# The last batch's dispatch weights made with tokens on the partitions, and the slots turned in two copies

## The chip, the cores and the metric

The kernel runs on one core of a Trainium2 chip. The metric is the device time of one execution in microseconds (us). The engines are TensorE (PE; its weight loads are PEld), VectorE (DVE), ScalarE (ACT), GpSimd (POOL) and SyncE (SP), which issues nearly all DMAs.

## The reference

Attention over 4 batches of 576 tokens, then a soft mixture of experts over all 2304 tokens, then an MLP with a Mish activation. What matters here is the dispatch of the mixture: each of the 32 slots takes a softmax over all tokens (over `axis 0`), and the slots' inputs are the weighted sums of the tokens.

```
x = attention(q, k, v)                      # (2304, 512)
logits = x @ phi                            # (2304, 32): a column for each slot
d = exp(logits - logits.max(0))             # maximum and sum run over the tokens
d /= d.sum(0) + 1e-9
slot_input = d.T @ x                        # (32, 512), 4 slots for each of 8 experts
h = relu(slot_input[e] @ w1[e]); slot_out[e] = h @ w2[e]
c = exp(logits - logits.max(1)); c /= c.sum(1) + 1e-9
y = c @ slot_out
out = (h2 * tanh(softplus(h2))) @ w_out     # h2 = y @ w_in
```

## The kernel before

The work runs in 16 periods, one for each pair of heads, in an order written out by hand (`PLAN`; `TAIL` for the last pair). Every recorded instruction of these stages keeps its place in its engine's queue, so an instruction that waits holds up all that stands behind it. After every fourth pair a batch is complete: its logits stand in `c_all[:, b]` with 128 tokens on the partitions, in 5 tiles of 32 slots (the fifth holds 64 tokens).

The softmax over tokens is kept running over the batches. For a batch the logits are turned on PE (`lt_pe`, tile `m_lt`, two halves), so that the 32 slots lie on the partitions; DVE takes their maxima (`lt_max`, tile `nM`, kept negated); ACT takes the exponentials and sums them (`lt_exp`, tile `lt`); DVE brings the running sum up to date (`lt_sum`, `asum`); PE turns the weights back (`d_pe`, tile `m_d`), and a copy takes them to `d`. `slots_pe` makes the weighted sums of the tokens (tile `m_si`: four products on `xg`, four on the rest `xr`, each in a quarter of the array's columns) and spreads the old sums' factor to 128 partitions (`m_al`). `slots_sum` adds them to the running slots in `acc`.

For the first three batches this lies inside the attention of the next batch. For the last one nothing is left beside it: the experts wait for the slots. The slots in `acc` are turned by four products (tile `m_sit`) and copied to `si_t`, which GpSimd has cleared. Then `h_ps` takes `si_t` times `w1`, 128 products in quarters of the array; after each, SP issues a load of a quarter of a `w2` matrix into the place of the weights just read (`quarter`). `rows_max`, `rows_less`, `rows_exp` make the combine weights of the last batch. `warm` issues products that nobody reads.

A single precision product of this kind stands in the trace as two records, a transposition as one.

Of the kernel before, what the change touches and what calls it, by code (L numbers as in the profile page):

```python
# [7 lines left out]
F32 = mybir.dt.float32  # L8
F32R = mybir.dt.float32r
U32 = mybir.dt.uint32  # L10
AF = mybir.ActivationFunctionType
ALU = mybir.AluOpType
# [30 lines left out]


TAIL = (
    "E8 y0 t5 T6 K1 T7 t6 k1 t7 R rA rD Q X0 qA qD B0 ca0 z1 w0 B1 B2 B3 B4 La la x1 Y1 X1 y1 ca1 Lb lb w1"
).split()


# [4 lines left out]
def kernel(  # L54
# [13 lines left out]
    nc = tc.nc  # L68
    NB, H, S, D = q.shape
    E, DM, F1 = w1.shape  # L70
    NSLOT = phi.shape[1]
# [3 lines left out]
    R = S - 512  # L75
    SCALE = 1.0 / float(D) ** 0.5
    KDM = DM // 128
# [7 lines left out]
    ps_m = psx.enter_context(tc.tile_pool(name="ps_m", bufs=4, space=PSUM))  # L85
# [11 lines left out]
    pe, act, dve, pool_, sp = (InOrder(e) for e in (nc.tensor, nc.scalar, nc.vector, nc.gpsimd, nc.sync))  # L97

    cs = const.tile([128, C_END], F32, name="cs")
    ident = cs[:, C_ID:C_ID + 128]  # L100
    rr = cs[:, C_RR:C_RR + 128]
    ii = cs[:, C_RR:C_RR + NSLOT]
# [4 lines left out]
    c_all = const.tile([128, NB, 5, NSLOT], F32, name="c_all")  # L107
    acc = const.tile([128, DM], F32, name="acc")

    nM = [const.tile([NSLOT, 3], F32, name=f"nM{i}") for i in range(2)]  # L110
    asum = const.tile([NSLOT, 2], F32, name="asum")
    asum4 = const.tile([128, 2], F32, name="asum4")
# [62 lines left out]
    def refill(keys):  # L175

        new = []
        for key in keys:
            room = parts.pop(key)
            if order[0][0] < 3:  # L180
                new.append(order.pop(0))
                parts[new[-1]] = room
            elif room[1][0] in (ra, rd):
                rooms.append(room[1])
        return new
# [25 lines left out]
    am = att.enter_context(tc.tile_pool(name="am", bufs=1))  # L211
# [15 lines left out]
    zs = [am.tile([128, 10, 2], F32, name=f"z{i}") for i in range(2)]  # L227
    sums = am.tile([NSLOT, 3], F32, name="sums")
    esum = sums[:, 1:3]
    tmps = [am.tile([128, 2 + i, 2, NSLOT], F32, name=f"tmp{i}") for i in range(2)]  # L230

    dma = sp.dma_start
# [10 lines left out]
    def load_pair(p, which="qk", dma=dma):  # L243
        b, h = divmod(2 * p, H)
        for nm in which:
            src = q if nm == "q" else k
            t = work(2, 2 * "qk".index(nm) + p % 2, (2, 256))
            dma(out=t, in_=src[b, h:h + 2, 0:512, :].rearrange("h (p c) d -> p h (c d)", c=4))
            raw[nm, p] = t
# [334 lines left out]
    dmat = {}  # L584

    def warm(pool, tag, n):

        ps = pool.tile([128, 128], F32, tag=tag, name="warm")
        for _ in range(n):
            tc.keep_in_program_order(nc.tensor.matmul(ps, lhsT=ident, rhs=ident, start=True, stop=True))  # L590

    def xtile(b, t):
        if t < 4:
            return xg[b, t // 2][:, t % 2, :]
        return xg[b, 2][:, :]
# [3 lines left out]
    def rows_max(b):  # L599
        st = rst[b] = am.tile([128, 5, 1], F32, tag="rst", name="rst")  # L600
        c = c_all[:, b]
        dve.tensor_reduce(out=st, in_=c, axis=AX.X, op=ALU.max)

    def rows_less(b):
        c = c_all[:, b]
        (dve if b == NB - 1 else pool_).tensor_tensor(out=c, in0=c, in1=rst[b].to_broadcast([128, 5, NSLOT]),
                                                      op=ALU.subtract)

    def rows_exp(b):
        act.activation(out=c_all[:, b], in_=c_all[:, b], func=AF.Exp)  # L610
# [27 lines left out]
    def lt_exp(b, i):  # L638
        new, nxt = nM[b % 2], nM[(b + 1) % 2]
        cur, old = nxt[:, 2:3], new[:, 2:3]  # L640
        if i == 0:
            dmat[b] = am.tile([NSLOT, S], F32, tag="lt", name="lt")
        o, n = HALVES[b][i]
        act.activation(out=dmat[b][:, o:o + n], in_=dmat.pop(("s", b, i))[:, 0:n], func=AF.Exp, bias=cur,
                       accum_out=esum[:, i:i + 1])
        if i and b:
            act.activation(out=asum[:, 0:1], in_=old, func=AF.Exp, scale=-1.0, bias=cur)

    def lt_sum(b):
        if b:  # L650
            dve.tensor_scalar(out=sums[:, 0:1], in0=asum[:, 1:2], scalar1=asum[:, 0:1], scalar2=None, op0=ALU.mult)
        dve.tensor_reduce(out=asum[:, 1:2], in_=sums[:, 0 if b else 1:3], axis=AX.X, op=ALU.add)

    def d_pe(b):
        lt = dmat.pop(b)
        ps = dmat["d", b] = ps_m.tile([128, 5, NSLOT], F32, tag="m", name="m_d")
        for t in range(5):
            n = 128 if t < 4 else R
            pe.transpose(ps[0:n, t, :], lt[:, t * 128:t * 128 + n], ident[0:NSLOT, 0:NSLOT])

    def d_copy(b, on, t0=None):
        if ("D", b) not in dmat:
            dmat["D", b] = am.tile([128, 5, NSLOT], F32, tag="d", name="d")
        d, ps = dmat["D", b], dmat["d", b]
        if on == "d" or t0 == 0:
            (dve.tensor_copy if on == "d" else act.copy)(d[:, 0:4], ps[:, 0:4])
        else:
            act.copy(d[0:R, 4], ps[0:R, 4])

    def slots_pe(b):  # L670
        dmat.pop(("d", b))
        d = dmat.pop(("D", b))
        al = None
        if b:
            al = ps_m.tile([128, 2], F32, tag="m", name="m_al")
            pe.matmul(al, lhsT=rr[0:NSLOT, :], rhs=asum, start=True, stop=True)
            dve.tensor_copy(asum4, al)
        ps = ps_m.tile([128, DM], F32, tag="m", name="m_si")
        for t in range(4):
            pe.matmul(ps[32 * t:32 * t + 32, :], lhsT=d[:, t, :], rhs=xtile(b, t), start=True, stop=False)  # L680
        for t in range(4):
            cols = slice(t * 128, (t + 1) * 128)
            pe.matmul(ps[32 * t:32 * t + 32, cols], lhsT=d[0:R, 4, :], rhs=xtile(b, 4)[:, cols],
                      start=False, stop=True)
        dmat["z", b] = ps
        for g in range(3):
            xg.pop((b, g))

    def slots_sum(b):
        ps = dmat.pop(("z", b))  # L690
        if b:
            n = DM // (2 if b == NB - 1 else 1)
            for o in range(0, DM, n):
                x, y = acc[:, o:o + n], ps[:, o:o + n]
                dve.scalar_tensor_tensor(out=x, in0=x, scalar=asum4[:, 0:1], in1=y, op0=ALU.mult, op1=ALU.add)
        else:
            dve.tensor_copy(acc, ps)

    pool_.memset(c_all, 0.0)
    dma(out=cs[:, C_COS:C_END], in_=cst[:, C_COS:C_END])  # L700
    load_pair(0, "k", act.dma_start)
    dma(out=cs[:, 0:C_COS], in_=cst[:, 0:C_COS])
# [200 lines left out]
    b = NB - 1  # L903
    ends = {"La": lambda: lt_pe(b, 0), "la": lambda: lt_max(b, 0), "Lb": lambda: lt_pe(b, 1), "lb": lambda: lt_max(b, 1)}
    for period in range(1, NP):
        for name, n in plan:
            p = period - n
# [6 lines left out]
    for name in TAIL:  # L914
        if name in ends:
            ends[name]()
        else:
            steps[name](NP - 1)
    warm(ps_m, "m", 6)
    lt_exp(b, 0)  # L920
    lt_exp(b, 1)
    lt_sum(b)
    d_pe(b)
    warm(ps_m, "m", 1)
    d_copy(b, "a", 4)
    d_copy(b, "a", 0)
    slots_pe(b)
    rows_max(b)
    rows_less(b)
    rows_exp(b)  # L930
    slots_sum(b)
    warm(ps_m, "m", 3)
    att.close()
    psx.close()

# [6 lines left out]
    ps_m = pse.enter_context(tc.tile_pool(name="ps_m2", bufs=6, space=PSUM, reuse_waits="tile"))  # L942

    si_t = p4.tile([128, KDM, 288], F32, name="si_t")
# [9 lines left out]
    for key in [take(rb, f"w{i}") for i in range(NRB)]:  # L954
        fetch(key)

    ps = ps_m.tile([128, KDM, NSLOT], F32, tag="m", name="m_sit")
    for c in range(KDM):
        nc.tensor.matmul(ps[:, c, :], lhsT=acc[:, c * 128:(c + 1) * 128], rhs=ii, start=True, stop=True)
    nc.vector.tensor_copy(  # L960
        si_t.rearrange("p c (e x) -> p c e x", x=36)[:, :, :, 0:4], ps.rearrange("p c (e j) -> p c e j", j=4)
    )

    warm(ps_m, "m", 1)

    rows_sum(b)
    rows_scale(b)
# [53 lines left out]
    for eg in range(2):  # L1021
        for hf in range(2):
            end = eg == 1 and hf == 1
            rows = [parts[1, 4 * eg + g, hf][0] for g in range(4)]
            new = refill([(1, 4 * eg + g, hf) for g in range(4)])
            for cc, fh in [(cc, fh) for cc in range(2) for fh in range(2)] if not end else [(0, 0), (1, 0), (0, 1), (1, 1)]:
                c = 2 * hf + cc
                for g in range(4):
                    e = 4 * eg + g
                    tc.keep_in_program_order(nc.tensor.matmul(  # L1030
                        h_ps[fh][32 * g:32 * g + 32, :], lhsT=si_t[:, c, 32 * e:32 * e + 32],
                        rhs=rows[g][:, cc * F1 + fh * 512:cc * F1 + fh * 512 + 512],
                        start=(eg == 0 and c == 0), stop=(eg == 1 and c == KDM - 1),
# [60 lines left out]
    for eg in range(2):  # L1094
        for hf in range(2):
            for cc in range(4):
                c = 4 * hf + cc
                for g in range(4):
                    e = 4 * eg + g
                    tc.keep_in_program_order(nc.tensor.matmul(  # L1100
                        so_ps[32 * g:32 * g + 32, :], lhsT=h_t[eg][:, c, 32 * g:32 * g + 32],
                        rhs=parts[2, e, hf][0][:, cc * DM:(cc + 1) * DM],
                        start=(eg == 0 and c == 0), stop=(eg == 1 and c == F1 // 128 - 1),
# [9 lines left out]
    for n, copy in ((0, nc.vector.tensor_copy), (2, nc.scalar.copy)):  # L1113
        ps = ps_m.tile([128, 2, 128], F32, tag="m", name="m_sot")
        for c in range(2):
            pin(nc.tensor.matmul(ps[:, c, :], lhsT=so_sb[:, (n + c) * 128:(n + c + 1) * 128], rhs=rr, start=True,
                                 stop=True))
# [395 lines left out]
    for u in range(len(units) + 2):  # L1513

        lag = 1 if u < UL else 2
        i, j = units[u] if u < len(units) else (None, None)
# [96 lines left out]
```

## Time and profile before

| | us |
|---|---|
| median of 3 runs | 581.66 |
| the 3 runs | 581.66, 581.52, 582.77 |
| the profiled execution's own time | 583.26 |
| its span, first to last instruction | 581.5 |
| mean granted clock of TensorE over the span | 0.996 |

The profiled execution took 1.76 us more than its span, and 1.60 us more than the median of the runs. A granted clock of 1.00 is 2.4 GHz, one of 0.50 is 1.2 GHz. The page gives busy time for each engine, a chain that is followed back from the last instruction, and groups of instructions. The rows below are from the stretch between the last pair of heads (to about 316 us) and the first expert products (from 325 us).

### The profile page before, as it was taken

The page shows a single profiled execution, that of the slowest core. Times are in us where ns is not written, and L with a number is a line of the kernel's source. Part 1 is how long each engine was busy: PE and PEld are TensorE (multiplying, and loading weights), DVE is VectorE, ACT ScalarE, POOL GpSimd, SP SyncE. Part 2 cuts the span into 40 slices and gives each one's busy share as a digit, 9 for nine tenths or more (in the row PEclk, how much of TensorE's full clock was granted, in tenths as well). Part 3 has the DMA queues.
Part 4 walks back from the last instruction along what each step waited for, and adds up shares of the span by engine and source line. Part 5 has one row for each costly group of instructions (what it writes and reads, how often), then busy time and mean ns, then how long its engine had stood idle before and what let it go on. Part 6 is the DMA issues. An engine that isn't in the chain of part 4 may idle for free.

```text
span 581.5 us, 12009 instructions
## 1 busy us (share of the span) xinstructions
PE 569.0 (98%) x4277; PEld 467.4 (80%) x4277; DVE 423.8 (73%) x867; ACT 389.1 (67%) x846; POOL 316.0 (54%) x399
## 2 busy tenths in 40 slices
PE   8899999999999999999998999999999999999996
PEld 7788887879888888878886435777788899999996
DVE  6787887988888878887574252999987756566564
ACT  4788887978888778886773032776757656556562
POOL 3968877689877777784000310000000078999993
PEclk9999999999999999999999999999999999999999
DMA  8599789999999888959877999642103010100112
GB/s 225 145 242 237 216 221 275 238 284 277 287 285 259 265 266 244 265 156 325 244 291 263 328 385 385 231 159 96 37 1 109 2 37 1 38 26 11 37 23 52
DMA packets 60475, 108.53 MB, mean 187 GB/s; under 512 B 13056, under 2 KB 26752, under 8 KB 60032
## 3 DMA queue, kind: packets, MB, share of 16 engines
q1 hardware_dynamic: 60144, 107.50, 61.7%
q8 instruction: 34, 0.56, 0.4%
q10 hardware_dynamic: 272, 0.26, 0.1%
q14 instruction: 25, 0.20, 0.1%
HBM read 70.25 MB, written 9.96 MB: 138 GB/s over the span
## 4 chain that ended last, share of the span: by engine, by line
PE 92%; DVE 4%; ACT 2%; DMA 1%; issue 1%; DVEq 0%; ACTq 0%
PE o_ps L1415 17%; PE s L95 15%; PE m_av L95 14%; PE o_ps L1313 14%; PE t L95 11%; PE hp L1238 3%; PE m_lg L95 3%; PE h_ps L1030 2%; PE so_ps L1100 2%; PE m_x L95 1%; PE m_q L95 1%; PE tk L95 1%; PE m_k L95 1%; PE m_si L95 1%; PE warm L590 1%; DMA w<-in_k_dram 1%
## 5 line engine op out<-in xcount | busy, mean ns | idle before, releaser
L1382 POOL TENSOR_TENSOR gr<-gr 128x128 f32<-128x128 f32 x81 | 59.8, 740 | 128.9 <-ACT gr L1378 124.5
L95 DVE TENSOR_REDUCE nmax<-s 128x1 f32<-128x576 f32 x144 | 107.0, 752 | 25.2 <-PE s L95 22.4
L95 ACT ACTIVATE P<-s,nmax 128x576 f32<-128x576 f32 x144 | 107.3, 746 | 17.3 <-DVE nmax L95 15.9
L95 PE MATMUL s<-qk_st 128*128 128x288 f32 x320 | 102.3, 337 | 1.9 <-ACT P L95 1.4
L1415 PE MATMUL o_ps<-ts,gr 128*128 128x256 f32 x480 | 97.5, 280 | 0.0
L95 POOL TENSOR_TENSOR w<-w,cs 128x512 f32<-128x512 f32 (+2 forms) x75 | 87.0, 1179 | 4.6 <-DMA w<-in_k_dram 2.6
L95 PE MATMUL s<-k_st,qk_st 128*128 128x288 f32 x320 | 89.1, 295 | 0.0
L95 PE MATMUL t<-cs,P 128*128 128x128 f32 x576 | 84.0, 273 | 0.0
L1415 PEld LDWEIGHTS o_ps<-ts,gr 128*128 128x128 f32 x480 | 80.0, 189 | 0.0
L95 PEld LDWEIGHTS s<-qk_st 128*128 128x128 f32 x320 | 60.3, 189 | 16.0 <-issue 9.1
L95 POOL TENSOR_TENSOR w<-w 128x256 f32<-128x256 f32 (+2 forms) x86 | 65.2, 779 | 13.6 <-ACT P L95 10.6
L95 ACT COPY PT<-t 128x512 f32<-128x512 f32 (+1 forms) x111 | 61.0, 558 | 14.0 <-PE t L95 12.5
L95 PEld LDWEIGHTS t<-cs,P 128*128 128x128 f32 x576 | 67.9, 142 | 1.4 <-DVE partl L95 0.6
L1415 PE MATMUL o_ps<-wo_h,gr 128*128 128x256 f32 x240 | 63.6, 283 | 0.0
L95 PEld LDWEIGHTS s<-k_st,qk_st 128*128 128x128 f32 x320 | 60.6, 190 | 0.0
L95 PE MATMUL m_av<-PT,w 128*64 128x320 f32 (+1 forms) x384 | 52.0, 411 | 0.0
L1313 PE MATMUL o_ps<-wo_h,gh 128*128 128x512 f32 x128 | 50.1, 394 | 0.0
L1313 PE MATMUL o_ps<-wo_l,gh 128*128 128x512 f32 x128 | 50.0, 393 | 0.0
L95 POOL TENSOR_TENSOR c_all<-c_all,tmp 128x64 f32<-128x64 f32 (+1 forms) x44 | 22.1, 502 | 50.3 <-DVE tmp L95 48.6
L1415 PEld LDWEIGHTS o_ps<-wo_h,gr 128*128 128x128 f32 x240 | 45.0, 188 | 0.2
L1398 DVE TENSOR_TENSOR gr<-gr 128x896 fp32r<-128x896 f32 (+2 forms) x28 | 31.4, 1122 | 17.4 <-ACT gr L1388 17.4
L95 PEld LDWEIGHTS m_av<-PT,w 128*64 128x64 f32 x384 | 25.8, 137 | 18.4 <-ACT PT L95 1.3
(208 smaller groups left out, 1192.1 us busy)
## 6 DMA issues: line engine op xcount, KB each, us to landing
w<-in_moe_w_dram SPq DMA_DIRECT2D x23, 1024.0 KB, 6.7
w<-in_moe_w_dram SPq DMA_DIRECT2D x36, 256.0 KB, 5.3
w<-in_moe_w_in_dram SPq DMA_DIRECT2D x16, 512.0 KB, 5.9
qk_st<-parth SPq DMA_DIRECT2D x45, 144.0 KB, 4.0
qk_st<-partl SPq DMA_DIRECT2D x45, 144.0 KB, 3.7
room<-in_moe_w_out_dram SPq DMA_DIRECT2D x12, 512.0 KB, 3.4
w<-in_q_dram SPq DMA_DIRECT2D x16, 256.0 KB, 4.3
w<-in_k_dram SPq DMA_DIRECT2D x15, 256.0 KB, 4.4
```

The lines of the kernel that those rows point to most:

```text
L95: return lambda *a, **k: tc.keep_in_program_order(f(*a, **k))
L590: tc.keep_in_program_order(nc.tensor.matmul(ps, lhsT=ident, rhs=ident, start=True, stop=True))
L1030: tc.keep_in_program_order(nc.tensor.matmul(h_ps[fh][32 * g:32 * g + 32, :], lhsT=si_t[:, c, 32 * e:32 * e + 32], rhs=rows[g][:, cc * F1 + ...
L1100: tc.keep_in_program_order(nc.tensor.matmul(so_ps[32 * g:32 * g + 32, :], lhsT=h_t[eg][:, c, 32 * g:32 * g + 32], rhs=parts[2, e, hf][0][: ...
L1238: pin(nc.tensor.matmul(hp[:, x * 256:x * 256 + 256], lhsT=wst[:, f * 128:(f + 1) * 128], rhs=ct[:, i * 256:(i + 1) * 256], start=True, sto ...
L1313: pin(nc.tensor.matmul(ops[i, n], lhsT=g_[:, cols], rhs=w_[f], start=(j == 0 and (x, k) == (0, 0)), stop=(j == NG - 1 and all(y[0] != n fo ...
L1382: pin(eng.tensor_tensor(out=o, in0=x, in1=y, op=op))
L1398: pin(nc.vector.tensor_tensor(out=l[:, x:y], in0=ga[u][:, 128 + x:128 + y], in1=h[:, x:y].bitcast(F32), op=ALU.subtract))
L1415: pin(nc.tensor.matmul(ops[p], lhsT=lhs, rhs=rhs, start=first, stop=(j == NG - 1 and k == 2)))
```

## The change

For the last batch alone, the logits are no longer exponentiated with slots on the partitions and turned back. The negated maxima of the 32 slots are spread to all 128 partitions by one product (`m_nm`: the maxima as weights, repeated 128 times, times a unit matrix). DVE adds them to `c_all` and ACT takes the exponentials in place, with the tokens on the partitions as the products of `m_si` need them. The slots' sums over the tokens are then made by GpSimd over the 5 tiles (`dsum`), copied four times side by side (`dsum4`) and summed over the partitions by a product with ones (`m_e`). The eleven `warm` products from `lt_pe` to `h_ps` become four. In `TAIL`, the step `w1` (scaling the last tokens into `xg` and `xr`) comes before `lb` (the maxima of the second half). The turned slots are made and copied in two parts, two column blocks by ACT and two by DVE.

```diff
-... ca1 Lb lb w1"
+... ca1 Lb w1 lb"
...
+    def last_weights(b):
+        new, nxt = nM[b % 2], nM[(b + 1) % 2]
+        cur, old = nxt[:, 2:3], new[:, 2:3]
...
+        warm(ps_m, "m", 1)
+        nm = ps_m.tile([128, NSLOT], F32, tag="m", name="m_nm")
+        pe.matmul(nm, lhsT=cur.to_broadcast([NSLOT, 128]), rhs=ident[0:NSLOT, 0:NSLOT], start=True, stop=True)
+        act.activation(out=asum[:, 0:1], in_=old, func=AF.Exp, scale=-1.0, bias=cur)
+        d = dmat["D", b] = am.tile([128, 5, NSLOT], F32, tag="d", name="d")
+        m = nm.rearrange("p (o s) -> p o s", o=1).to_broadcast([128, 5, NSLOT])
+        dve.tensor_tensor(out=d, in0=c_all[:, b], in1=m, op=ALU.add)
+        act.activation(out=d, in_=d, func=AF.Exp)
+        al = ps_m.tile([128, 2], F32, tag="m", name="m_al")
+        pe.matmul(al, lhsT=rr[0:NSLOT, :], rhs=asum, start=True, stop=True)
+        dve.tensor_copy(asum4, al)
+        warm(ps_m, "m", 1)
+
+    def last_slots(b):
+        d = dmat.pop(("D", b))
+        slots_products(b, d)
+        pool_.tensor_tensor(out=dsum, in0=d[:, 0:2], in1=d[:, 2:4], op=ALU.add)
+        pool_.tensor_tensor(out=dsum[:, 0], in0=dsum[:, 0], in1=dsum[:, 1], op=ALU.add)
+        pool_.tensor_tensor(out=dsum[0:R, 0], in0=dsum[0:R, 0], in1=d[0:R, 4], op=ALU.add)
+        dmat["e", b] = e = ps_m.tile([128, 2], F32, tag="m", name="m_e")
+        pool_.tensor_copy(dsum4.rearrange("p (o s) -> p o s", s=NSLOT),
+                          dsum[:, 0:1].to_broadcast([128, 4, NSLOT]))
+        pe.matmul(e, lhsT=dsum4, rhs=ones, start=True, stop=True)
+
+    def last_sums(b):
+        x = asum4[:, 1:2]
+        dve.scalar_tensor_tensor(out=x, in0=x, scalar=asum4[:, 0:1], in1=dmat.pop(("e", b))[:, 0:1], op0=ALU.mult,
+                                 op1=ALU.add)
...
-    warm(ps_m, "m", 6)
-    lt_exp(b, 0)
-    lt_exp(b, 1)
-    lt_sum(b)
-    d_pe(b)
-    warm(ps_m, "m", 1)
-    d_copy(b, "a", 4)
-    d_copy(b, "a", 0)
-    slots_pe(b)
+    last_weights(b)
     rows_max(b)
     rows_less(b)
     rows_exp(b)
+    last_slots(b)
     slots_sum(b)
-    warm(ps_m, "m", 3)
+    last_sums(b)
+    warm(ps_m, "m", 2)
...
-    ps = ps_m.tile([128, KDM, NSLOT], F32, tag="m", name="m_sit")
-    for c in range(KDM):
-        nc.tensor.matmul(ps[:, c, :], lhsT=acc[:, c * 128:(c + 1) * 128], rhs=ii, start=True, stop=True)
-    nc.vector.tensor_copy(
-        si_t.rearrange("p c (e x) -> p c e x", x=36)[:, :, :, 0:4], ps.rearrange("p c (e j) -> p c e j", j=4)
-    )
-
-    warm(ps_m, "m", 1)
+    for c, copy in ((0, nc.scalar.copy), (2, nc.vector.tensor_copy)):
+        ps = ps_m.tile([128, 2, NSLOT], F32, tag="m", name="m_sit")
+        for j in range(2):
+            tc.keep_in_program_order(nc.tensor.matmul(
+                ps[:, j, :], lhsT=acc[:, (c + j) * 128:(c + j + 1) * 128], rhs=ii, start=True, stop=True))
+        tc.keep_in_program_order(copy(
+            si_t[:, c:c + 2].rearrange("p c (e x) -> p c e x", x=36)[:, :, :, 0:4],
+            ps.rearrange("p c (e j) -> p c e j", j=4)))
```

On PE, between the last turning of the logits and the first expert product, these instructions stood before the change (`m_lt` to `m_sit` as above; a row's figures are its output's shape and how many follow each other):

```order
L95 MATMUL m_lt<-cs,c_all 32x128 x2
L95 MATMUL m_lt<-cs,c_all 32x64
L590 MATMUL warm<-cs 128x128 x6
L95 MATMUL m_d<-cs,lt 128x32 x4
L95 MATMUL m_d<-cs,lt 64x32
L590 MATMUL warm<-cs 128x128
L95 MATMUL m_al<-asum,cs 128x2
L95 MATMUL m_si<-xg,d 32x512 x4
L95 MATMUL m_si<-xr,d 32x128 x4
L590 MATMUL warm<-cs 128x128 x3
L959 MATMUL m_sit<-cs,acc 128x32 x4
L590 MATMUL warm<-cs 128x128
```

The same place on PE with the change:

```order
L95 MATMUL m_lt<-cs,c_all 32x64
L593 MATMUL warm<-cs 128x128
L95 MATMUL m_nm<-cs,nM_70 128x32
L95 MATMUL m_al<-asum,cs 128x2
L593 MATMUL warm<-cs 128x128
L95 MATMUL m_si<-xg,d 32x512 x4
L95 MATMUL m_si<-xr,d 32x128 x4
L95 MATMUL m_e<-ones,dsum_128 128x2
L593 MATMUL warm<-cs 128x128 x2
L997 MATMUL m_sit<-cs,acc 128x32 x4
```

The five transpositions `m_d` and seven `warm` products are gone; `m_nm` and `m_e` are new, and `m_e`, which waits for GpSimd, stands ahead of the last two `warm` products and of `m_sit`.

On DVE, from the logits of the last tile on, this stood before the change:

```order
L95 TENSOR_TENSOR c_all<-c_all,tmp_127 128x96 x2
L95 TENSOR_REDUCE nM_71<-m_lt 32x1
L95 TENSOR_REDUCE nM_70<-nM_71 32x1
L95 TENSOR_TENSOR xg<-m_x,rz 128x2x128
L95 TENSOR_TENSOR xr<-m_x,rz 64x128
L95 TENSOR_SCALAR sums<-asum 32x1
L95 TENSOR_REDUCE asum<-sums 32x1
L95 COPY asum_73<-m_al 128x2
```

The same place on DVE with the change:

```order
L95 TENSOR_TENSOR c_all<-c_all,tmp_130 128x96 x2
L95 TENSOR_TENSOR xg<-m_x,rz 128x2x128
L95 TENSOR_TENSOR xr<-m_x,rz 64x128
L95 TENSOR_REDUCE nM_71<-m_lt 32x1
L95 TENSOR_REDUCE nM_70<-nM_71 32x1
L95 TENSOR_TENSOR d<-c_all,m_nm 128x160
L95 COPY asum_73<-m_al 128x2
```

The two scalings `xg` and `xr` moved ahead of the maxima, the two small steps of the running sum left, and the addition that makes `d` came in.

On GpSimd, the four steps of the sums stand ahead of the clearing of `si_t`, which was the first instruction of this stretch before:

```order
L95 TENSOR_TENSOR dsum<-d 128x64
L95 TENSOR_TENSOR dsum<-dsum 128x32
L95 TENSOR_TENSOR dsum<-dsum,d 64x32
L95 COPY dsum_128<-dsum 128x128
L987 MEMSET si_t 128x1152
```

Both copies into `si_t` stand behind that clearing.

## Rows read from the trace of the kernel before

**Rows 1.** The page: the engines' busy time, and the chain's shares by engine.
```profile
PE 569.0 (98%) x4277; PEld 467.4 (80%) x4277; DVE 423.8 (73%) x867; ACT 389.1 (67%) x846; POOL 316.0 (54%) x399
...
PE 92%; DVE 4%; ACT 2%; DMA 1%; issue 1%; DVEq 0%; ACTq 0%
```

**Rows 2.** The chain that ended last, 312 to 328 us: start, us, what.
```profile
317.04 0.14 issue
317.17 0.54 PE m_lt L95 x3
317.71 2.84 PE warm L590 x12
320.55 0.61 PE m_d L95 x5
321.16 0.42 PE warm L590 x2
321.58 0.31 PE m_al L95 x2
321.89 1.35 PE m_si L95 x16
323.24 0.87 PE warm L590 x6
324.10 0.83 PE m_sit L959 x8
...
325.03 0.30 DVE si_t L960
325.37 2.76 PE h_ps L1030 x21
```

**Rows 3.** Timeline of DVE, ACT and POOL, 313.3 to 326.2 us: start, us, what.
```profile
317.75 0.48 DVE L95 TENSOR_REDUCE nM<-m_lt 32x1 f32<-32x320 f32 x1 [0.72 <-PE m_lt L95]
318.26 0.14 DVE L95 TENSOR_REDUCE nM<-nM 32x1 f32<-32x3 f32 x1
318.33 0.40 DVE L95 TENSOR_TENSOR xg<-m_x,rz 128x256 f32<-128x256 f32 x1
318.77 0.29 DVE L95 TENSOR_TENSOR xr<-m_x,rz 64x128 f32<-64x128 f32 x1
...
322.35 0.33 DVE L95 TENSOR_TENSOR c_all<-c_all,rst 128x160 f32<-128x160 f32 x1
...
323.31 0.87 DVE L95 SCALAR_TENSOR_TENSOR acc<-acc,asum,m_si 128x256 f32<-128x256 f32 x2 [0.56 <-PE m_si L95]
...
318.96 0.50 ACT L95 ACTIVATE lt<-m_lt,nM 32x320 f32<-32x320 f32 x1
...
322.71 0.34 ACT L95 ACTIVATE c_all<-c_all 128x160 f32<-128x160 f32 x1 [1.17 <-DVE c_all L95]
...
322.98 1.06 POOL L950 MEMSET si_t<- 128x1152 f32 x1 [19.61 <-PE m_si L95]
```

**Rows 4.** Busy time in three stretches; PEclk is the granted clock.
```profile
314.29:317.70 3.41, 2.10 (x17) 1.33 (x15) 1.45 (x5) 0.43 (x1) 0.00 (x0) 1.00 1.02 389
317.70:321.12 3.42, 3.42 (x19) 3.13 (x18) 1.59 (x6) 1.25 (x5) 0.00 (x0) 0.50 1.05 390
321.12:324.54 3.42, 3.42 (x34) 2.25 (x33) 1.70 (x7) 0.68 (x3) 1.56 (x2) 1.00 1.05 387
```

**Rows 5.** Groups of GpSimd by form: busy us, mean ns of one.
```profile
L1382 POOL TENSOR_TENSOR gr<-gr 128x128 f32<-128x128 f32 x81 | 59.8, 740 | 128.9 <-ACT gr L1378 124.5
...
L95 POOL TENSOR_TENSOR c_all<-c_all,tmp 128x64 f32<-128x64 f32 x22 | 8.4, 382 | 8.3 <-DVE tmp L95 7.4
...
L980 POOL COPY phi_sb<-c_all 128x128 f32<-128x128 f32 x4 | 1.2, 293 | 0.0
```

**Rows 6.** Two later stretches, same columns; the last two are the DMA share and GB/s.
```profile
326.00:328.00 2.00, 2.00 (x26) 0.55 (x20) 0.33 (x1) 0.00 (x0) 1.04 (x3) 1.00 0.23 67
328.00:366.00 38.00, 37.59 (x321) 16.76 (x314) 13.97 (x34) 11.21 (x29) 2.55 (x6) 1.00 1.04 383
```

More of the change, by code (lines that the diff above doesn't have):

```diff
@@ L45 @@
 TAIL = (
-    "E8 y0 t5 T6 K1 T7 t6 k1 t7 R rA rD Q X0 qA qD B0 ca0 z1 w0 B1 B2 B3 B4 La la x1 Y1 X1 y1 ca1 Lb lb w1"
+    "E8 y0 t5 T6 K1 T7 t6 k1 t7 R rA rD Q X0 qA qD B0 ca0 z1 w0 B1 B2 B3 B4 La la x1 Y1 X1 y1 ca1 Lb w1 lb"
 ).split()
@@ L229 @@
     esum = sums[:, 1:3]
+    ones = am.tile([128, 2], F32, name="ones")
+    dsum = am.tile([128, 2, NSLOT], F32, name="dsum")
+    dsum4 = am.tile([128, 128], F32, name="dsum4")
     tmps = [am.tile([128, 2 + i, 2, NSLOT], F32, name=f"tmp{i}") for i in range(2)]
@@ L677, in slots_pe, with slots_products @@
             dve.tensor_copy(asum4, al)
+        slots_products(b, d)
+    def slots_products(b, d):
         ps = ps_m.tile([128, DM], F32, tag="m", name="m_si")
@@ L687, in slots_pe @@
             xg.pop((b, g))
+    def last_weights(b):
+        new, nxt = nM[b % 2], nM[(b + 1) % 2]
+        cur, old = nxt[:, 2:3], new[:, 2:3]
+        for i in range(2):
+            dmat.pop(("s", b, i))
+        warm(ps_m, "m", 1)
[12 more added lines that the diff above has]
+        d = dmat.pop(("D", b))
+        slots_products(b, d)
+        pool_.tensor_tensor(out=dsum, in0=d[:, 0:2], in1=d[:, 2:4], op=ALU.add)
[9 more added lines that the diff above has]
+                                 op1=ALU.add)
     def slots_sum(b):
@@ L699 @@
     pool_.memset(c_all, 0.0)
+    pool_.memset(ones, 1.0)
     dma(out=cs[:, C_COS:C_END], in_=cst[:, C_COS:C_END])
```

## The prediction, made before the change was run

> **What bounds the kernel now.** I read the page first. PE is busy 98% of the span and the chain of waits lies on it for 92% [rows 1], so nothing is won by taking work from another engine unless PE waits for it. The change touches one stretch, from the last turning of the logits to the first expert product, and there the chain has to be read step by step [rows 2]. After `m_lt` ends at 317.71 us come twelve `warm` records, `m_d`, more `warm` and `m_al`, `m_si` from 321.89, `warm`, `m_sit`, a copy by DVE, and `h_ps` at 325.37. That is 7.66 us in which only the short steps are needed work.
>
> The third view is the granted clock. It is 0.50 from 317.70 to 321.12 and 1.00 on either side; ahead of the fall PE was busy 2.10 of 3.41 us [rows 4]. So the `warm` records ran at 1.2 GHz: twelve took 2.84 us, 0.237 each, where six later ones at 2.4 GHz took 0.87, 0.145 each [rows 2]. At full clock the twelve would have ended at 317.71 + 1.74 = 319.45, and ACT's second exponential ends at 319.46 [rows 3]. `m_d` could have begun about 319.5 instead of 320.55: the low clock cost this execution about 1.05 us.
>
> That bears on what is compared. The profiled execution took 583.26 us, the median run 581.66. Two of the three runs lie at 581.5 to 581.7 and one 1.1 us above, which is about that price. I therefore take the median run to be one in which the clock did not fall, and `h_ps` to begin there at 325.37 - 1.05 = 324.32 on the profile's scale. The other 0.55 us of the 1.60 between profile and median I cannot place.
>
> **The change, step by step.** I keep the profile's time scale, from the end of `m_lt` at 317.71.
>
> The two scalings `xg` and `xr` (0.40 and 0.29 us [rows 3]) now stand between the logits and the maxima. The logits are done at 317.04 [rows 2], so the scalings end at 317.80 with their gaps, 0.05 later than the maximum began before (317.75 [rows 3]). They fill DVE's wait for `m_lt`; that is the cost of the move in `TAIL`. The two maxima take 0.48 and 0.14 [rows 3] and end at 318.47.
>
> PE gets its word 0.14 later, as it did between logits and `m_lt` [rows 2]. No row shows `m_nm`, a two-record product of 32 columns; the nearest is `m_al`, 0.31 for two records [rows 2]. With its drain I take 0.4: 319.0. The lower bound is 0.3, the upper 0.6 (`m_d`, five records). DVE's addition is a 128x160 operation like the subtraction in 0.33 [rows 3], here from PSUM: 319.4. ACT's exponential of 128x160 takes 0.34 [rows 3]: 319.78. `m_si` begins at 319.83 instead of 321.89, with no turning back, no accumulator reads and no copies of `d`.
>
> From there two paths run. The first is `m_si`, 1.35 us at full clock [rows 2], to 321.18; half of the additions into `acc` (half of 0.87 [rows 3]); then 0.14 to PE: `m_sit` could begin at 321.85. The second is new. GpSimd's four steps have no row of their own. Its 128x64 addition takes 0.38, its 128x128 copy 0.29 [rows 5]; with two smaller additions at 0.3 and three hand-overs of 0.05 the four take 1.4 us and end at 321.3. If every addition took the 0.74 of a 128x128 one [rows 5], it is 2.7 us; if small ones cost next to nothing, 0.8. I take 1.4, since the sizes are at or under 128x64. Then `m_e` (0.14 + 0.3) and the four `warm` records queued behind it (4 x 0.145) let `m_sit` start at 322.3. The second path is the later one; part of its hand-over lies under the PE queue, so I take 322.15.
>
> GpSimd then clears `si_t` in 1.06 [rows 3], 321.3 to 322.4, which before ran under the additions and now ends just ahead of its first reader. That reader is ACT's copy after four of the eight `m_sit` records (half of 0.83 [rows 2], 0.2 drain): 322.77. The copy takes under the 0.30 of DVE's whole one [rows 2]: `h_ps` at 323.1. It waits for ACT's half alone; DVE's half is first read 16 products later. The steps of the running sum are needed only by the scaling after the `h_ps` products, so they cost nothing; without that cover, three small DVE steps would cost about 0.5.
>
> At full clock in both kernels the gain is 324.32 - 323.1 = 1.2 us.
>
> Does it reach the end? From 328 to 366 us DMA is full (share 1.04), and between 326 and 328 nearly idle (0.23) [rows 6], since the `w2` loads are issued by the `h_ps` products. An earlier `h_ps` brings that stream forward, and there are about 1.5 us of idle to move it into. So up to 1.5 us pass through.
>
> **The clock in the changed kernel.** Between 317.04 and 319.83 PE now has `m_lt` (0.54), two `warm` products and two tiny ones, about 1.6 us of work in 2.8; before that stretch it was no busier [rows 4]. Before, six `warm` products filled the wait. I expect the clock to fall in most executions of the changed kernel, again for some 3.4 us [rows 4]. What that costs depends on where it lies. If it covers all of `m_si`, its 1.35 us double; if it ends before 319.8, nothing. The last `warm` records add up to 0.4. I take 0.6, half of 1.2. So against the median: 581.66 - 1.2 + 0.6 = 581.06, say **581.0 us**.
>
> Against the profiled execution, with the clock as it was: `m_si` runs 1.29 us at half speed to 321.12, ends at 321.82, and `h_ps` begins about 323.45, so 1.9 us earlier, 581.35 on that execution's own scale.
>
> [...]
>
> **Rivals.** A measurement of this kernel can tell about 0.2% (1.16 us) from no change.
>
> *The clock falls in neither kernel, or in the changed one where it costs nothing.* The gain is the whole 1.2: 580.5, just at the bound. For it: two of three runs seem undisturbed. Against: the sparse stretch is wider now.
>
> *The median of before has the low stretch, as the profiled execution had.* Then like is compared with like, 1.9 us: 579.8. For it: the only trace there is shows it. Against: the 1.1 us between the runs.
>
> *GpSimd holds up PE.* `m_e` waits in order ahead of `m_sit`. With 2.7 us for the sums, they end at 322.5, `m_sit` starts at 323.5 and `h_ps` at 324.4: the gain at full clock is gone, 581.7.
>
> *The clock stays low into the expert products.* If it stays at 1.2 GHz as long again, to 324.5, `m_si` and `warm` lose all they gained: about 581.7. If it lasts a third such stretch, to 327.9, about 3.4 us of `h_ps` run at half speed, another 1.7: 583.4. This decides from some 2.3 us of low clock inside `h_ps` on. For it: the missing `warm` products. Against: the clock rose at 321.12 after one such stretch, and `m_si` and `h_ps` are dense.
>
> **How the numbers follow.** Forecast 0.46 (own range 580.4 to 581.6); no cost from the clock 0.18; low stretch in before 0.18; GpSimd late or a second low stretch 0.10; low into the experts 0.08. Faster by over 0.2% (under 580.5): half of the second case, the third, and a tail of the first, 0.33. Slower (over 582.8): the last, 0.08. Within: 0.59. The range, 579.6 to 582.3, leaves out the last case, a little of the third, and what I overlooked.
>
> **What would show it.** In the profile after: `m_si` about 2 us after the end of `m_lt`; `m_e` within 2 us of ACT's exponential; ACT's copy into `si_t` waiting for PE and not for GpSimd's clearing; `h_ps` 5.4 to 6.2 us after `m_lt` instead of 7.66; a granted clock of 0.50 that begins between 317 and 320 and is over before `h_ps`; DMA idle for under 1.5 us before the full stretch. The forecast is wrong if the clock stays at 1.00 through `m_si`, if it is low in `h_ps`, or if `m_sit` waits for `m_e`.

## The result and the profile after

The changed kernel takes 585.37 us (median of 22 runs, 584.35 to 587.02); the kernel before takes 581.84 (22 runs beside them, 581.23 to 587.45). The ratio is 1.0057, 95% interval 1.0046 to 1.0067: slower by 0.6%. The forecast was 581.0, with a range of 579.6 to 582.3. Three executions of 799 to 1238 us, in e9 and e10 below, were disturbed as a whole and are left out of every median and ratio.

The profiled execution took 585.12 us, its span is 583.3 and its mean granted clock 0.991. The page first: PE's share and the chain's are those of [rows 1], but one slice of forty has a lower clock.

```profile
PE 570.4 (98%) x4262; PEld 466.2 (80%) x4262; DVE 424.5 (73%) x867; ACT 388.3 (67%) x842; POOL 317.3 (54%) x404
...
PEclk9999999999999999999999699999999999999999
...
PE 92%; DVE 4%; ACT 2%; DMA 1%; issue 1%; DVEq 0%; ACTq 0%
```

The same stretch by windows, where PEclk is the third figure from the end and DMA's share the second. It answers to [rows 4].

```profile
316.33:319.75 3.42, 2.45 (x17) 1.53 (x19) 2.48 (x9) 0.76 (x3) 0.40 (x1) 1.00 1.03 383
319.75:323.16 3.41, 3.41 (x25) 2.03 (x17) 1.32 (x5) 0.21 (x1) 3.06 (x6) 0.50 1.05 397
323.16:326.58 3.42, 3.42 (x19) 1.82 (x22) 1.14 (x5) 0.21 (x1) 1.84 (x3) 0.50 0.78 290
326.58:329.99 3.41, 3.41 (x20) 0.79 (x16) 0.00 (x0) 0.00 (x0) 0.00 (x0) 0.50 0.82 225
329.99:333.40 3.41, 3.41 (x36) 0.96 (x32) 0.00 (x0) 0.00 (x0) 0.00 (x0) 1.00 0.98 336
```

The clock is 0.50, that is 1.2 GHz, from 319.75 to 329.99: 10.24 us, where before it was 3.42 [rows 4]. The last two rows hold nothing but `h_ps` products: 20 in 3.41 us at the low level, 36 at the full one. A PE that is "busy" for the whole of a row may do little more than half the work.

Next the timeline of PE, GpSimd and ACT, an instruction group per row (start, us, what, and in brackets the idle time ahead and what ended it).

```profile
316.66 0.54 PE L95 MATMUL m_lt<-cs,c_all 128*32 128x128 f32 x3 [1.05 <-DVE c_all L95]
317.13 0.49 PE L593 MATMUL warm<-cs 128*128 128x128 f32 x2
318.13 0.37 PE L95 MATMUL m_nm<-cs,nM 32*128 32x32 f32 x2 [0.51 <-DVE nM L95]
...
319.31 0.40 POOL L95 TENSOR_TENSOR dsum<-d 128x64 f32<-128x64 f32 x1 [16.45 <-ACT d L95]
...
320.42 0.29 POOL L95 COPY dsum<-dsum 128x128 f32<-128x128 f32 x1
...
320.89 1.06 POOL L987 MEMSET si_t<- 128x1152 f32 x1 [0.18 <-PE m_si L95]
...
323.76 0.21 ACT L999 COPY si_t<-m_sit 128x64 f32<-128x64 f32 x1 [3.80 <-PE m_sit L997]
```

And the chain that ended last, which answers to [rows 2].

```profile
316.55 0.42 DVE xg L95
...
317.00 0.29 DVE xr L95
...
317.33 0.49 DVE nM L95
...
317.84 0.16 DVE nM L95
318.00 0.14 issue
318.13 0.39 PE m_nm L95 x2
...
318.54 0.33 DVE d L95
...
318.90 0.34 ACT d L95
...
319.29 2.11 PE m_si L95 x16
321.40 0.52 PE m_e L95 x2
321.92 1.06 PE warm L593 x4
322.98 1.55 PE m_sit L997 x8
```

The chain then goes on in `h_ps`; here are its first 64 records (one for each product), with the change and, below, before.

```profile
324.52 9.73 PE h_ps L1067 x64
```

```profile
325.37 7.07 PE h_ps L1030 x64
```

Until `m_si` it is short: `m_lt` ends at 317.20 and `m_si` begins at 319.29, 2.09 us later, where before it was 4.18 [rows 2]. From there on everything runs at the low clock: `m_si` 2.11 us instead of 1.35, `m_sit` 1.55 instead of 0.83.

Where did the 1.8 us between the two profiled spans come from? `m_lt` ended 0.51 us earlier (317.20, not 317.71), in the part that the change does not touch. From there to `h_ps` it took 7.32 us instead of 7.66. From `h_ps` to the end it took 258.8 instead of 256.1. So the kernel gained 0.3 us, less than its shorter chain is worth, ahead of `h_ps`, and lost 2.7 behind, at a place whose instructions are the same: its first 64 records took 9.73 us instead of 7.07. That fits 5.47 us of `h_ps` (324.52 to 329.99) at half speed.

### The profile page after: what moved, and what is told of

The parts are those of the page before. It is cut to its first block, busy times and chain, and to the rows that moved or that the text cites. A ratio compares the mean times of both kernels' runs of the same rounds, so it can differ in the third digit from the quotient of the medians.

```text
span 583.3 us, 11982 instructions
## 1 busy us (share of the span) xinstructions
PE 570.4 (98%) x4262; PEld 466.2 (80%) x4262; DVE 424.5 (73%) x867; ACT 388.3 (67%) x842; POOL 317.3 (54%) x404
## 4 chain that ended last, share of the span: by engine, by line
PE 92%; DVE 4%; ACT 2%; DMA 1%; issue 1%; DVEq 0%; ACTq 0%
PE o_ps L1452 17%; PE s L95 15%; PE m_av L95 14%; PE o_ps L1350 14%; PE t L95 11%; PE hp L1275 3%; PE h_ps L1067 3%; PE m_lg L95 3%; PE so_ps L1137 2%; PE m_x L95 1%; PE m_q L95 1%; PE tk L95 1%; PE m_k L95 1%; PE m_si L95 1%; DVE w L95 1%; DMA w<-in_k_dram 1%
## 6 DMA issues: line engine op xcount, KB each, us to landing
w<-in_moe_w_dram SPq DMA_DIRECT2D x36, 256.0 KB, 5.3
w<-in_q_dram SPq DMA_DIRECT2D x16, 256.0 KB, 4.0
w<-in_k_dram SPq DMA_DIRECT2D x15, 256.0 KB, 4.4
```

## The experiments

The theories. **C**: the clock. The change opens waits on PE and takes seven `warm` products out; the clock falls, and stays low through the chain and into `h_ps`. **G**: GpSimd. The sums by GpSimd and the wait of `m_e` for them hold PE up. The last column of the table counts executions with a mean granted clock of 0.998 or more over the span. By the profiles, one low stretch of 3.4 us makes it 0.996 (before), 6.8 us 0.993 or 0.994, 10.2 us 0.991, 13.7 us 0.987 or 0.988.

| kernel | `warm` products | median us | ratio to before, 95% | full clock |
|---|---|---|---|---|
| the change | 4 | 585.37 | 1.0057 [1.0046, 1.0067] | 0 of 22 |
| e1_warm_as_before | 11 | 582.12 | 1.0000 [0.9974, 1.0026] | 9 of 11 |
| e2_before_few_warm | 4 | 586.34 | 1.0072 [1.0057, 1.0088] | 0 of 6 |
| e3_waits_filled | 10 | 581.05 | 0.9979 [0.9970, 0.9987] | 11 of 11 |
| e4_sums_off_the_path | 4 | 583.43 | 1.0037 [1.0019, 1.0056] | 2 of 12 |
| e5_fill_ahead_of_lt | 8 | 581.05 | 1.0002 [0.9979, 1.0024] | 7 of 12 |
| e6_fill_ahead_of_nm | 6 | 585.50 | 1.0034 [1.0007, 1.0061] | 4 of 12 |
| e7_four_in_the_waits | 4 | 583.66 | 1.0013 [0.9994, 1.0031] | 3 of 12 |
| e8_filled_and_sums_off_the_path | 10 | 581.75 | 0.9978 [0.9962, 0.9995] | 11 of 11 |
| e9_dense_late | 10 | 585.28 | 1.0042 [1.0017, 1.0067] | 1 of 10 |
| e10_filled_one_copy | 10 | 581.64 | 0.9965 [0.9938, 0.9992] | 11 of 11 |
| e11_filled_none_behind_sums | 8 | 580.94 | 0.9964 [0.9943, 0.9985] | 10 of 12 |
| e12_filled_one_copy_again | 10 | 581.50 | 0.9977 [0.9960, 0.9994] | 12 of 12 |

The kernel before ran beside each of them: beside e1 to e4 with a median of 582.26 and the full clock in 22 of 29 executions, beside e5 to e8 with 582.26 and 29 of 35, beside e9 to e11 with 582.59 and 17 of 28, beside e12 with 582.33 and 13 of 17. Its executions at full clock alone have medians of 582.10, 582.18, 582.25 and 582.25. The ratio is not the quotient of the two medians (e5: 581.05 and 582.26, but 1.0002); executions that lost the clock enter it on both sides. Small differences at full clock are therefore taken below between the executions with full clock.

### The warm products given back, and taken from the kernel before

e1 puts the counts of before into the changed kernel; e2 puts the few of the change into the kernel before.

```diff
 e1, on the changed kernel
-        warm(ps_m, "m", 1)
+        warm(ps_m, "m", 6)
         nm = ps_m.tile(
...
-    warm(ps_m, "m", 2)
+    warm(ps_m, "m", 3)
...
+    warm(ps_m, "m", 1)
     rows_sum(b)
 e2, on the kernel before
-    warm(ps_m, "m", 6)
+    warm(ps_m, "m", 1)
     lt_exp(b, 0)
...
-    warm(ps_m, "m", 3)
+    warm(ps_m, "m", 2)
...
-    warm(ps_m, "m", 1)
     rows_sum(b)
```

Expected of e1: 

> Theory C (the clock): the changed kernel lost its time because PE, with four useless products instead of eleven, stayed at 1.2 GHz into the expert products. Rival G (GpSimd and the new order): m_e, which waits for GpSimd's sums ahead of m_sit, and the clearing of si_t behind those sums hold the experts back. Here all eleven products are back at their places (six, one, three, one), everything else as changed. C: the granted clock is back at 1.00 before the experts, h_ps begins 0.4 to 1.2 us sooner after m_lt than in the kernel before, 580.8 to 582.5 us. G: the wait for m_e stays, 584.5 us or more.

Expected of e2: 

> The kernel before with the changed kernel's number of useless products (one, one, two, none) and nothing else changed. C: the clock falls and stays at 0.50 into h_ps for 4 us or more, 584.5 to 586.5 us. G: nothing of GpSimd is in the way here, the shorter queue helps or does nothing, 580.5 to 582 us.

e1 takes 582.12, as before, though GpSimd makes the sums and `m_e` stands behind them just as in the changed kernel. It is no faster than before because the `warm` products now hold the chain up: `m_nm` begins 1.53 us behind `m_lt` (318.03 to 319.56, against 0.93 in the changed kernel), and `h_ps` 6.39. e2 takes 586.34, though it has neither GpSimd's sums nor `m_e`: the kernel before gets slower than the changed one by the loss of seven `warm` products alone. The waits of e2 name GpSimd once, the clearing of `h_t` ahead of DVE's copy into `si_t` (326.38). But that copy began 0.11 us after the end of `m_sit`, the same as before the change, and there it began at 325.03, 1.2 us ahead of the end of that clearing; so it does not need it. G falls as the cause of the loss; C holds in both directions. The windows of e2:

```profile
317.02:320.43 3.41, 2.65 (x12) 1.72 (x10) 1.59 (x6) 1.58 (x7) 0.00 (x0) 0.50 1.05 393
...
327.26:330.67 3.41, 3.41 (x20) 0.79 (x16) 0.39 (x2) 0.00 (x0) 0.00 (x0) 0.50 0.30 73
330.67:334.08 3.41, 3.41 (x36) 0.96 (x32) 0.00 (x0) 0.00 (x0) 0.00 (x0) 1.00 1.01 324
```

The clock is low from 317.02 to 330.67, 13.65 us, and the last of it lies in `h_ps` with the same 20 records in 3.41 us as in the changed kernel.

### The waits filled, both or one of them

PE waits twice in the changed kernel between the logits and `m_si`: 1.05 us ahead of the last `m_lt` and 0.51 ahead of `m_nm`. e3 fills both, e5 the first, e6 the second; e7 has the change's four `warm` products, but all in the two waits. In its profile 0.61 and 0.29 us are left of these, and waits of 0.54 and 0.15 us have opened ahead of `m_si` and `m_sit`.

```diff
 e3; e5 has the first two edits, e6 the third
-... x1 Y1 X1 y1 ca1 Lb w1 lb"
+... x1 Y1 X1 y1 ca1 warm Lb w1 lb"
...
+            "warm": lambda: warm(ps_m, "m", 4)}
...
-        warm(ps_m, "m", 1)
+        warm(ps_m, "m", 3)
         nm = ps_m.tile(
 e7: as e3 with 2 and 2, and without these
         dve.tensor_copy(asum4, al)
-        warm(ps_m, "m", 1)
...
     last_sums(b)
-    warm(ps_m, "m", 2)
```

Expected of e3: 

> The changed kernel with useless products put where PE waits anyway: four between the turning of the last tokens (m_x) and the last m_lt, three instead of one ahead of m_nm. C: the clock does not fall at all or not into h_ps, and the shorter chain shows: h_ps 5.4 to 6.2 us after the last m_lt ended, 580.0 to 581.2 us. G: 584.5 to 586 us as the changed kernel.

Expected of e5: 

> The changed kernel with four more warm products in the wait ahead of the last turning m_lt (PE waits 1.05 us there in the changed kernel), and still one ahead of m_nm (0.51 us of wait); eight in all. If the long wait ahead of m_lt is what lets the clock fall (theory P1): the granted clock stays at or near 1.00 and the time is 581.0 to 581.5, h_ps 5.2 to 5.4 us after m_lt. If the wait between m_lt and m_nm is (P2): 0.50 for about 10 us and 584.5 to 585.5. If the number of warm products counts and not their place (N): between the two, nearer to 582, as eight is nearer to the eleven of before than to four.

Expected of e6: 

> The changed kernel with three warm products ahead of m_nm instead of one, nothing in the wait ahead of m_lt; six in all. P1 (the wait ahead of m_lt decides): still 0.50 for 7 to 10 us, 584 to 585.5. P2 (the wait between m_lt and m_nm decides): clock 1.00, 580.9 to 581.5. N (number): 584 to 585, as six is nearer to four. The kernel before has the wait ahead of m_lt unfilled too and loses its clock in some executions for 3.4 us, so a mixture of executions with none and with one such stretch, about 582, would say that both waits count.

Expected of e7: 

> The changed kernel with the same four warm products, but all of them in the two waits: two ahead of the last m_lt, two ahead of m_nm, none ahead of m_si and none behind m_e. N (number): 585, as in the changed kernel. P (place): clock at or near 1.00, and with no warm records left ahead of m_sit, which took 0.55 us in the kernel with filled waits, 580.5 to 581.2; in executions in which the clock still falls, one stretch of 3.4 us, 1 us more.

PE's timeline of e3, which stands against the changed kernel's first three rows above:

```profile
316.55 1.06 PE L593 MATMUL warm<-cs 128*128 128x128 f32 x8
317.77 0.54 PE L95 MATMUL m_lt<-cs,c_all 128*32 128x128 f32 x3 [0.16 <-DVE c_all L95]
318.24 0.94 PE L593 MATMUL warm<-cs 128*128 128x128 f32 x6
319.24 0.37 PE L95 MATMUL m_nm<-cs,nM 32*128 32x32 f32 x2
```

The wait ahead of `m_lt` shrinks from 1.05 to 0.16 us, the one ahead of `m_nm` to under 0.1, and none of the eleven executions lost its clock: 581.05, 1.2 us under the kernel before and faster than both kernels. Nor did any of the 34 of e8, e10 and e12 below, which fill both waits in the same way.

With one wait filled the kernel is of two minds. e5 gave 580.57 to 581.08 in the seven executions with full clock, and 584.1 to 585.9 in the five others; e6 580.6 to 581.4 in four and 585.0 to 587.5 in eight. So neither P1 nor P2 is right alone: both waits count. e7 has no more `warm` products than the changed kernel, and 3 of its 12 executions keep the clock where 0 of 22 did; its median is 583.66. e9 below has ten like e3, but six of them behind the fall, and keeps it in 1 of 10 where e3 does in 11 of 11. So place counts at the same number. What isn't refuted is the number *ahead of `m_si`*, whichever wait it fills: with two there (the change, e2, e4, e9) 3 of 50 executions have the full clock, with four (e6, e7) 7 of 24, with six (e5) 7 of 12, with seven (e1) 9 of 11, with eight (e3, e8, e10, e11, e12) 55 of 57. And e1 leaves the first wait of 1.05 us unfilled. What is shown is the share of executions, and that the same program has both outcomes; what decides in a single execution, no run shows.

e5 has a second use. Behind `m_lt` it is the changed kernel to the instruction, and its profiled execution had the full clock. The end of its chain:

```profile
321.52 0.38 PE m_e L95 x2
321.90 0.55 PE warm L593 x4
322.46 0.81 PE m_sit L998 x8
323.27 0.98 PE h_ps L1068 x5
```

`m_lt` ended at 317.95, so `h_ps` begins 5.32 us behind it. That is what the change does at full clock.

### GpSimd's sums taken off the path

e4 moves `m_e` and the last step of the running sum behind `m_sit` (`ones` and `dsum4` get other places in memory for it); e8 does the same in e3.

```diff
-        pe.matmul(e, lhsT=dsum4, rhs=ones, start=True, stop=True)
...
 def last_sums(b):
+    dmat["e", b] = e = ps_m.tile([128, 2], F32, tag="m", name="m_e")
+    pe.matmul(e, lhsT=dsum4, rhs=ones, start=True, stop=True)
...
     slots_sum(b)
-    last_sums(b)
     warm(ps_m, "m", 2)
...
+    last_sums(b)
     rows_sum(b)
```

Expected of e4: 

> The changed kernel with m_e and the three DVE steps behind it moved behind m_sit and its copies, so that neither PE nor DVE waits for GpSimd's sums ahead of the experts; the number of useless products stays at four. C: m_sit comes 0.3 to 0.9 us sooner, but the clock stays low into h_ps as before, 584.3 to 585.4 us. G: most of the loss comes back, 581 to 582.5 us.

Expected of e8: 

> The kernel with filled waits (e3_waits_filled, 581.05) and with the product m_e and the last step of the running sum behind m_sit, so that neither PE nor m_sit waits for GpSimd's sums. In the trace of e3_waits_filled m_sit starts 0.84 us after the end of m_si; additions into acc let it start at about 0.6. If GpSimd's sums hold m_sit: 0.2 to 0.3 us less than e3, 580.7 to 580.9. If they don't (m_sit waits for acc and si_t's clearing anyway): 581.0 to 581.1. If moving m_e alone had kept the clock up in the earlier kernel, nothing more is to be had here, since the waits are filled already.

e4 came out between the theories, 583.43: two executions with full clock (581.35 and 582.07), five of 582.5 to 583.5 at clocks of 0.993 to 0.996, five of 585.8 to 587.0 at 0.990 and less. The move shortens the low stretch in some executions; why, no run tells, since up to the end of `m_si` PE's program is that of the changed kernel. Where the clock is full, e8 shows what the wait for GpSimd costs: nothing that can be seen. In its profile `m_lt` ends at 318.05 and `h_ps` begins at 323.44, 5.39 us later, no sooner than in e3 (5.32): `m_e` now stands ahead of `h_ps` instead of ahead of `m_sit`. Its time is 0.7 above that of e3, 581.75 against 581.05 (0.6 when each is taken from the full-clock executions of before; the ratios in the table do not tell them apart); 256.6 us from `h_ps` to the end against 256.1 make most of it, and that difference arises in the last stage, behind the experts. e4's profile, at full clock and with the same buffers moved, has 256.7, from the same stage. Whether the moved buffers cause it was not tried.

### Work behind the fall

e9 leaves the waits as they are and puts eight `warm` products behind `m_e` in place of two.

```diff
     last_sums(b)
-    warm(ps_m, "m", 2)
+    warm(ps_m, "m", 8)
```

Expected: 

> The changed kernel with eight warm products behind m_e instead of two: the waits ahead of m_nm stay as empty as they are, and the clock will have fallen by then, as in the changed kernel (0.50 from 319.75). What brings it back is asked. Theory K (the kind of work: the warm products, which use the whole array without a pause, raise the clock, as in the kernel before, where it rose at 321.12 after twelve warm records; the quarter products of m_si, m_sit and h_ps do not do so as soon): it is 1.00 again before or within the first 2 us of h_ps, a low stretch of 3.4 or 6.8 us instead of 10.2, and h_ps to the end takes 256 to 257 us instead of 258.9. The twelve more records cost 1.7 us at full clock, 2.8 at half, less 0.3 that m_sit waits anyway: 584.5 to 586. Theory T (once fallen in this stretch, the clock stays low for about 10 us, whatever PE does): 0.50 for 10 us or more, the products cost 2.5 us on top and h_ps loses about as much less as it starts later: 586.5 to 588.

```profile
315.98:319.39 3.41, 1.89 (x11) 1.37 (x11) 2.62 (x11) 0.46 (x2) 0.00 (x0) 1.00 1.04 387
319.39:322.80 3.41, 3.29 (x20) 1.15 (x20) 1.03 (x4) 0.50 (x2) 2.34 (x6) 0.50 1.05 398
322.80:326.21 3.41, 3.41 (x18) 3.41 (x17) 0.71 (x4) 0.00 (x0) 2.10 (x2) 0.50 1.00 371
326.21:329.62 3.41, 3.41 (x33) 1.60 (x35) 1.13 (x5) 0.21 (x1) 0.84 (x2) 1.00 0.20 37
```

The low stretch is 6.82 us here, and the clock is back at 326.21, ahead of `h_ps` (327.11), after 3.6 us of `warm` records. From `h_ps` to the end it takes 256.1 us again. So T falls: the stretch has no fixed length. The profile is not alone: six of the ten executions have a mean clock of 0.993 or more, and none of the 22 of the changed kernel; but four lie at 0.987 to 0.991, so the products do not shorten the stretch every time. The time, 585.28, is that of the changed kernel, because the `warm` records cost on the chain what `h_ps` gets back.

K's figures all came out. But its reason, that the quarter products do not raise the clock as soon, is not shown by that. In five profiles the clock came back while PE ran `h_ps`: 5.5 us after its start in the changed kernel, 3.9 in e2, 4.9 in e6 and e7, 5.5 in e11. In the kernel before it came back after 2.8 us of `warm` records and the five of `m_d`, in e9 after 3.6 us of `warm` records. Both do it, and the times lie too near each other to tell the kinds apart. What did not is the stretch of `m_si`, `m_e`, four `warm` records and the start of `m_sit`, though its rows show PE busy throughout (3.41 of 3.41 us in the changed kernel from 319.75 to 323.16). A busy time that is full does not tell whether the clock will rise.

### The two copies, and the last warm products

e10 is e3 with `m_sit` in one tile and one copy by DVE, as before the change; its profile shows nothing of this stretch, so e12 is the same kernel once more. e11 is e3 without the two `warm` products behind `m_e`.

```diff
 e10, e12
-    for c, copy in ((0, nc.scalar.copy), (2, nc.vector.tensor_copy)):
...
+    ps = ps_m.tile([128, KDM, NSLOT], F32, tag="m", name="m_sit")
...
+    nc.vector.tensor_copy(
 e11
     last_sums(b)
-    warm(ps_m, "m", 2)
```

Expected of e10: 

> The kernel with filled waits (e3_waits_filled, 581.05) with the turned slots in one tile and one copy by DVE, as before the change. If the split into two copies is worth what the rows say (h_ps started 0.08 us ahead of the end of m_sit's eighth record, where a whole copy by DVE takes 0.30 and two hand-overs): h_ps 0.4 to 0.55 us later after m_lt, 5.65 to 5.8 us, and 581.4 to 581.6. If the split hides behind something else (GpSimd's clearing of si_t, a load): no change, 581.0.

Expected of e12: 

> The same kernel as e10_filled_one_copy, whose profiled execution fell on a disturbed clock (0.655 over its whole span) and shows nothing of the stretch. With a full clock: h_ps 5.65 to 5.8 us after the end of m_lt instead of the 5.25 of e3_waits_filled, its wait ended by DVE's one copy of 0.30 us, and 581.4 to 581.7 again. If the split had hidden behind something: h_ps at 5.25 to 5.4 us.

Expected of e11: 

> The kernel with filled waits without the two warm products behind m_e (eight in all: four ahead of m_lt, three ahead of m_nm, one ahead of m_si). If the warm records are what holds m_sit (they took 0.55 us behind m_e): m_sit starts 0.2 to 0.3 us sooner, bound by the additions into acc, and the copy by ACT is then bound by GpSimd's clearing of si_t, which ended 0.45 us ahead of it; 580.75 to 580.9 with the clock at 1.00. If the wait that opens between m_e and m_sit lets the clock fall as the two other waits did: executions of 583 to 586 among them, as in e5_fill_ahead_of_lt (5 of 12).

The end of e12's chain, and the same place in e3's:

```profile
322.49 0.83 PE m_sit L997 x8
...
323.41 0.30 DVE si_t L998
...
323.76 2.33 PE h_ps L1066 x17
```

```profile
322.81 0.81 PE m_sit L998 x8
323.63 3.34 PE h_ps L1068 x29
326.97 6.22 DMA w<-in_moe_w_dram
```

`m_lt` ended at 317.99 in e12, so `h_ps` began 5.77 us later, against 323.63 - 318.31 = 5.32 in e3: the two copies are worth 0.45 us. The medians, 581.64 and 581.50 against 581.05, say the same; taken from the full-clock median of before beside each, they are 0.61 and 0.75 us below it, and e3 is 1.05, so 0.3 to 0.4. In e3's chain the copy no longer shows, but a load of weights does, 3.3 us into `h_ps`: what is gained here beyond this may be spent on waiting for DMA.

e11 has `m_sit` at 322.54 and `h_ps` at 324.19 in a profile with a low clock from 322.86 on. Two of twelve executions (584.27, 584.76) lost the clock; the ten others lie at 580.39 to 581.27, median 580.82, against 581.05 for e3. The gain of 0.2 us (0.4 against the full-clock executions of before) lies within the scatter. The lost executions do not: without the two products the clock falls in some executions even with both waits filled.

## Why the prediction was wrong

**The median of before.** It was taken to be at full clock, and the price of the low stretch to be 1.05 us. The first was right as far as the record shows, the second of the right size. The runs beside the changed kernel have no clocks on record; beside e5 to e8, 29 of 35 executions of before had a clock of 0.998 or more, median 582.18, and the five at 0.996 or 0.997 have 583.68, 1.5 us more (beside the others 1.1 to 1.2). One lost more, 587.40. The 1.05 leaves out that `m_d` (0.61 us, 320.55 to 321.16) ran at the low level too.

**The chain to `m_si`.** Right. Forecast was 2.12 us from the end of `m_lt`; measured 2.09, with 0.39 for `m_nm` (0.4), 0.33 for the addition (0.33 from [rows 3]), and 0.34 for the exponential (0.34). The scalings hid in the wait as forecast, but for 0.1: `xr` ends at 317.29 and the first maximum starts at 317.33, 0.13 us after `m_lt`.

**GpSimd.** Right: the four sums run from 319.31 to 320.71, 1.40 us. At full clock PE waits 0.07 us for them (in e5 `m_si` ends at 321.45, `m_e` starts at 321.52). The copy by ACT waits for `m_sit`, not for the clearing of `si_t`.

**To `h_ps`, at full clock.** Forecast 5.39 us from the end of `m_lt`, measured 5.32 in e5. The last step was another than forecast: ACT's copy began 0.45 us behind the start of `m_sit` (322.46 to 322.91; the forecast had 0.62, of which 0.2 for a drain that no run shows), took 0.21 and was done at 323.12, and `h_ps` followed the last record of `m_sit` at 323.27. Against the 6.61 of before at full clock (an estimate, 7.66 - 1.05; no profile has that kernel at full clock) the chain is 1.3 us shorter (forecast 1.2). It reached the end: the seven executions of e5 with full clock have a median of 580.81, 1.4 us under the 582.18 of before.

**The clock in the changed kernel.** This is the step that failed. It was forecast to fall in most executions, "again for some 3.4 us", at a cost of 0.6 us. It fell in all 22, and for 10.24 us in the profile; the mean clocks of the 22, 0.987 to 0.991, fit stretches of 10 to 14 us. It was still low in `h_ps`, which the prediction had named as a sign that it is wrong, and `h_ps` began 7.32 us behind `m_lt`, not 5.4 to 6.2. What it costs can be read against e5. From `m_lt` to `h_ps` 7.32 us instead of 5.32, that is 2.0, of which `m_si` (2.11 for about 1.4), `warm` (1.06 for 0.55) and `m_sit` (1.55 for 0.81) make nearly all; from `h_ps` to the end 258.8 instead of 256.1, that is 2.7. The sum of 4.7 turns the 1.3 gained into 3.4 lost; measured are 3.5 (585.37 - 581.84).

The length was read from [rows 4] without asking what PE did until the clock rose there. The stretch was full of twelve `warm` records, ten of which the change takes out (six products there become one). That these products make the difference, e1 and e2 show. The argument against the last rival, that "`m_si` and `h_ps` are dense", did not hold: the clock stayed low through `m_si`, whose rows show no idle time, and rose only 5.47 us into `h_ps` (3.9 to 5.5 in the five profiles). So the last rival, at 0.08, was what happened. Its price was too small as well: 583.4 counted 1.7 us of `h_ps` and the gain of 1.2. Measured are 2.7, since the clock fell 2 us later than assumed (319.75, not 317.70) and so stayed low further into `h_ps`; and 2.0, since `m_sit`, `m_e` and the `warm` records pay double too.

The Trainium skill, "TensorE: Matmul & The Clock Gate", Part 1, says that the low clock is the default and that activity releases it. The runs agree with the direction: e1, e2 and e3 differ from their parents in nothing but products that keep PE active, and gain or lose 3 to 4.5 us by them. How much activity it takes they do not tell: PE shows as busy for all of the 10.24 us at the low clock.

**DMA.** The idle time of DMA ahead of its full stretch could take the gain, as forecast. At the low clock this could not be seen; in e5 and e3 the time from `h_ps` to the end is 256.0 and 256.1, as before.

## What to carry to other kernels

Products that nobody reads may carry the clock. Before taking them out of a chain, see which wait each of them fills, and price the clock for the work *behind* that chain, at the same instructions' half speed: here 1.3 us of shorter chain were paid with 4.7. When a chain gets shorter, keep the filler in the waits that are left (e3: 581.05, faster than both kernels), and look at the granted clock of every execution, since the same program can have both outcomes. The length of a low stretch in one trace holds only for the work that ran in it there.

## What the runs showed of the hardware

The changed kernel, with waits of 1.05 and 0.51 us and 0.54 us of products and a `warm` product between them, lost the clock in 22 of 22 executions; e4 and e9, the same on PE to the end of `m_si`, kept it in 3 of 22. With either wait filled it was lost in 5 or 8 of 12. With both filled it was lost in none of 45 (e3, e8, e10, e12), but in 2 of 12 when the two products behind `m_e` were gone (e11). And PE at 100% busy did not bring it back at once: in the changed kernel it stayed at 1.2 GHz for 10.24 us, in which the windows show no idle time at all.
